# Moving weight forms, conversions, chunk-end sums, evacuations and seeds in a Fourier-mixing and gated-FFN kernel

## Chip, cores and metric

The kernel runs on one core of one Trainium2 chip. The metric is the device time of one execution in microseconds; the median of three runs is given. The engines are called TensorE (PE in the profile; PEld is its weight load), VectorE (DVE), ScalarE (ACT), GpSimd (POOL) and SyncE (SP, which issues most DMAs).

## What is computed

The reference is a Fourier mixing of eight sequences of 3008 tokens with 256 features, followed by a gated feed-forward layer:

```python
X = np.fft.fft(x, axis=1)            # x: (8, 3008, 256)
X = np.fft.fft(X, axis=2)
y = X.real.astype(np.float32).reshape(8 * 3008, 256)
gate = 1.0 / (1.0 + np.exp(-(y @ w_gate)))     # w_gate, w_val: (256, 1536)
val = y @ w_val
out = (gate * val @ w_out).astype(np.float32)  # w_out: (1536, 256)
```

The weights arrive as 64-bit floats, so the kernel converts them to 32 bits itself; everything is computed in 32-bit floats.

## The kernel before

**The mixing.** The transform over the features is merged into the gate and value weights (`merge`, giving G1 and G2), so that the sequence transform alone is left per batch. It uses symmetry: x is folded (`fold_ops`), then multiplied by a table of cosines and sines (`seq_group`, `whole`), giving the parts pk and qk of a spectrum of 1505 positions. A position k and its mirror S-k have the same two products with opposite signs, so a gate or value at k is P + Q and at S-k it is P - Q.

**The main loop.** The 1505 positions are cut into six chunks of 252 (the last is 246), for each of eight batches. A chunk meets 12 tiles of 128 hidden units, so there are 48 chunks of 12 steps, 576 steps i in all. In step i the program emits, in this order:

- `front_a(i)`: two products with pk into a PSUM bank PF[i], two matmuls each. From step 12 on the bank was *seeded* before, by ScalarE (`seed`, L501), with the part of the outcome that is of rank one.
- `gate_a(i-1)`: ScalarE's sigmoid for position k (L534, into h) and VectorE's z for position S-k (L536 or L539).
- `part(i)`: the copy ae of PF[i], by ScalarE (L515) from step 12 on and by VectorE (L518) before. `front_b(i)` adds to the same bank, so it waits for ae.
- `gate_b(i-1)`: gate times value at k on VectorE (L551), the S-k sigmoid on ScalarE (L552), their product on VectorE (L553), and, after the second and third tile of a group of three, seven and six *h sums* on GpSimd (L558).
- the uses of weights due in this step (`use`): merges of gate and value weights on TensorE, evacuated to G2 and G1 by ScalarE; for output weights that complete a group, `forms(g)`.
- `back`: five of the fifteen products of an earlier group with the output weight forms, into the PSUM banks po0 to po4.
- `front_b(i)`: two products with qk.
- then the ScalarE half of a weight conversion (`weight_parts`, L260 and L261), the seed of step i+2, up to three items of the list `later`, and last the side work: VectorE's and GpSimd's half of a conversion (`weight_join`, L270 to L273, L275), weight loads, folds of the next batch's x on GpSimd, sequence groups.

A group of three hidden tiles is one level of a bilinear scheme: 15 products in place of 18, paid for by the h sums, by sums of the output weights (`W_SUMS`, eleven, and four copies per group, made once), and by 20 sums of the outcome at the end of each chunk (`C_SUMS`, L604). `back` works on group p five to seven steps after its first tile.

**At the end of a chunk** the banks po0 to po4 are copied to the tile c as they complete (L582), then `finish` puts 20 sums, four transposes (L612) and the stores into `later`, from where three go out per step. The first three go out in step 4 of the next chunk (counted from 0), the last in step 11. After the last chunk all of this is emitted at once, from a list of its own (`C_LAST`) whose entries also name the engine.

**What sets the order.** The program order above is each engine's order; nothing is rescheduled. Each engine works through its own list and waits where an operand, or a buffer to be written, isn't ready. PF has three banks, h three buffers, z, ae and sf two, c one. The weight jobs j run from 0 to 17 (gate, value and output weights by pairs of hidden tiles): job j >= 9 is converted in step j-9; gate and value pairs are merged two or three steps after that, and the output weights of groups 0 to 3 are formed in steps 3, 5, 9 and 11.

Of the kernel before, what the change touches and what calls it, by code (L numbers as in the profile page):

```python
# [11 lines left out]
ALU = mybir.AluOpType  # L12
# [49 lines left out]
PRODUCTS = ((0, 12), (1, 11), (4, 9), (6, 4), (2, 13), (5, 5), (13, 0), (8, 6), (11, 2), (12, 8), (9, 3),  # L62
            (10, 10), (14, 1), (15, 7), (16, 14))
PLACE = (0, 1, 2, 5, 3, 4, 6, 7, 8, 9, 10, 11, 14, 13, 12)
C_SUMS = (((8, 1, 8, 0), (1, 1, 0, 0), (3, 3, 1, 0), (0, 0, 10, 1), (4, 4, 0, 1), (1, 6, 2, 0),
           (4, 4, 1, 0), (10, 14, 8, 1), (7, 7, 10, 0), (11, 0, 11, 0), (11, 11, 5, 0), (5, 5, 7, 1)),
          ((9, 9, 8, 0), (9, 13, 9, 1), (9, 9, 2, 0), (12, 9, 12, 0), (12, 11, 12, 1), (14, 9, 14, 0),
           (6, 11, 6, 0), (13, 13, 6, 1)))
OUT = (3, 12)

C_LAST = (((8, 1, 8, 0), 0), ((1, 1, 0, 0), 0), ((3, 3, 1, 0), 0), ((1, 6, 2, 0), 1), ((0, 0, 10, 1), 0),
          ((11, 0, 11, 0), 1), ((4, 4, 0, 1), 0), ((4, 4, 1, 0), 0), ((11, 11, 5, 0), 1),
          ((9, 9, 8, 0), 1), ((10, 14, 8, 1), 0), ((7, 7, 10, 0), 0), ((6, 11, 6, 0), 1),
          ((5, 5, 7, 1), 0), ((9, 13, 9, 1), 0), ((9, 9, 2, 0), 0), ((14, 9, 14, 0), 0),
          ((13, 13, 6, 1), 0), ((12, 9, 12, 0), 0), ((12, 11, 12, 1), 0))
HUGE = float((2 ** 24 - 1 - 2 ** 20) * 2.0 ** -7)


@with_exitstack
def kernel(  # L80
# [174 lines left out]
    def weight_parts(j):  # L255

        if j in RAW:
            raw, ws = RAW[j], WS[j]
            lo, hi = raw[:, :, :, 0], raw[:, :, :, 1]
            nc.scalar.activation(ws, hi.bitcast(F32), AF.Abs)  # L260
            nc.scalar.activation(lo, lo.bitcast(U32), AF.Copy, scale=2.0 ** -29)  # L261

    def weight_join(j):
        if j not in RAW:
            return
        raw, ws = RAW.pop(j), WS[j]
        lo, hi = raw[:, :, :, 0], raw[:, :, :, 1]
        wi = ws.bitcast(I32)
        ts = nc.vector.tensor_scalar
        ts(out=ws, in0=ws, scalar1=2.0 ** -15, scalar2=HUGE, op0=ALU.max, op1=ALU.min)  # L270
        ts(out=wi, in0=wi, scalar1=3, scalar2=0x3FFFFFF8, op0=ALU.logical_shift_left,
           op1=ALU.bitwise_and)
        nc.vector.scalar_tensor_tensor(out=wi, in0=hi, scalar=-(2 ** 30), in1=wi,  # L273
                                       op0=ALU.bitwise_and, op1=ALU.bitwise_or)
        nc.gpsimd.tensor_tensor(wi, wi, lo, op=ALU.add)  # L275

    WO = {}

    def weight_use(j, other=None):
        w, c = jobs[j]  # L280
        if w == 2:
            WO[c] = WS.pop(j)
            for g in range(NG):
                if (3 * g + 2) // 2 == c:
                    forms(g)
        else:
            merge(WS.pop(j), w, c, other)

# [13 lines left out]
    def forms(g):  # L302

        w = [WO[f // 2].rearrange("p f (a h j) -> p f h a j", h=2, j=TB)[:, f % 2]
             for f in range(3 * g, 3 * g + 3)]
        f = wf[:, g].rearrange("p m (a j) -> p m a j", j=TB)

        def block(i):
            return w[i // 2][:, i % 2] if i < 6 else f[:, i - 6]
        for i, (a, b, op) in enumerate(W_SUMS):  # L310
            nc.gpsimd.tensor_tensor(f[:, i], block(a), block(b), op=(ALU.subtract, ALU.add)[op])  # L311
        for i, (a, sign) in enumerate(W_COPIES):
            nc.scalar.mul(f[:, len(W_SUMS) + i], block(a), float(sign))


    W = {}
# [224 lines left out]
    def block(p, i):  # L541

        R = 2 * chunks[groups[p][1]][1] // 3
        return H[p][:, i % 3, i // 3 * R : (i // 3 + 1) * R] if i < 9 else SF[p][:, i - 9, 0:R]
# [20 lines left out]
    def back(p, part):  # L565

        b, c, g = groups[p]
        n = chunks[c][1]
        R = 2 * n // 3
        last = p == len(groups) - 1  # L570
        if part == 0 and g == 0:
            PO[:] = [pso.tile([P, 2 * WC], F32, name=f"po{t}", tag=f"po{t}") for t in range(NB)]
        for at_, (hb, wb) in list(enumerate(PRODUCTS))[part * 5 : part * 5 + 5]:
            t, j = divmod(PLACE[at_], 3)
            mm(PO[t][:, j * R : (j + 1) * R], wf[:, g, wb], block(p, hb), g == 0 and at_ % 3 == 0,
               g == NG - 1)
            if g == NG - 1 and at_ % 3 == 2:
                if t == 0:
                    C[0] = cp.tile([P, 10 * WC], F32, name="c", tag="c")
                    nc.gpsimd.memset(C[0][:, 15 * R : 15 * R + 40], 0.0)  # L580
                if not (last and t == NB - 1):
                    nc.scalar.copy(C[0][:, 3 * t * R : 3 * (t + 1) * R], PO[t][:, 0 : 3 * R])  # L582
        if part == 2:
            del H[p], SF[p]
            if g == NG - 1:
                finish(b, c, last)

    def finish(b, c, last):
        k0, n = chunks[c]
        R = 2 * n // 3  # L590
        more = k0 + n > NK
        nb = -(-n // TB)
        t = C.pop(0)
        queues = (nc.sync, nc.scalar) if last else (nc.sync,)
        os_ = []

        new = set()

        def sum_(dst, a, b, op, engine=nc.vector):

            there = lambda i: last and i >= 3 * (NB - 1) and i not in new
            v = [PO[NB - 1][:, (i - 3 * NB + 3) * R : (i - 3 * NB + 4) * R] if there(i) else
                 t[:, i * R : (i + 1) * R] for i in (a, b)]
            engine.tensor_tensor(t[:, dst * R : (dst + 1) * R], *v, op=(ALU.subtract, ALU.add)[op])  # L604
            new.add(dst)

        def flip(s, h):
            if not os_:
                os_.append(op.tile([P, NK + 1], F32, name="os", tag="os")[:, 0 : 4 * WC].rearrange(
                    "p (s b h j) -> p s b h j", s=2, h=2, j=TB))  # L610
            c0 = OUT[h] * R + (n + more if s else 0)
            nc.vector.transpose(os_[0][:, s, 0:nb, h, :], t[:, c0 : c0 + nb * TB])  # L612

        def store(s):
            m, r0 = (min(n, M - k0), b * S + k0) if s == 0 else (
                n - (k0 == 0) - more, b * S + S - k0 - n + 1 + more)
            full = m // TB
            for a in range(4):
                ps = slice(a * TB, (a + 1) * TB)
                cs = slice(a * 2 * TB, (a + 1) * 2 * TB)  # L620
                queues[a % len(queues)].dma_start(
                    out=out[r0 : r0 + full * TB, cs].rearrange("(b t) d -> t b d", t=TB),
                    in_=os_[0][ps, s, 0:full].rearrange("p b h j -> p b (h j)"))
                if m > full * TB:
                    queues[a % len(queues)].dma_start(out=out[r0 + full * TB : r0 + m, cs],
                                      in_=os_[0][a * TB : a * TB + m - full * TB, s, full].rearrange(
                                          "p h j -> p (h j)"))

        if last:
            for x, e in C_LAST:  # L630
                sum_(*x, engine=(nc.vector, nc.gpsimd)[e])
                if x[0] == 5:
                    flip(0, 0)
                    flip(1, 0)
            for half in range(2):
                flip(half, 1)
                store(half)
            return
        for h in range(2):
            later.extend([lambda x=x: sum_(*x) for x in C_SUMS[h]])  # L640
            later.append(lambda h=h: flip(0, h))
            later.append(lambda h=h: (flip(1, h), h and (store(0), store(1))))

# [49 lines left out]
    def at(i, *fs):  # L695
        side.setdefault(i, []).extend(fs)
# [2 lines left out]

    pre, use = {}, {}  # L700
    for j in range(9, len(jobs)):
        pre.setdefault(j - 9, []).append(lambda j=j: weight_parts(j))
        at(j - 9, lambda j=j: weight_join(j))
        if KEEP <= j < len(jobs) - 3:
            at(j - 9, lambda j=j: weight_load(j + 3))
    for j in range(3, len(jobs)):
# [40 lines left out]
    for i in range(count):  # L747
        front_a(i)
        if i:
            gate_a(i - 1)  # L750
        part(i)
        if i:
            gate_b(i - 1)
        for f in use.pop(i, []):
            f()
        if i >= 5:
            back((i - 5) // 3, (i - 5) % 3)
        front_b(i)
        for f in pre.pop(i, []):
            f()  # L760
        for j in range(max(i0, i + 1), min(count, i + 3)):
            if j not in PF:
                seed(j)
        for f in later[0:3]:
            f()
        del later[0:3]
        for f in side.pop(i, []):
            f()
# [55 lines left out]
```

## Time and profile before

| | |
|---|---|
| median of 3 runs (lowest to highest) | 1994.02 us (1992.43 to 1995.59) |
| span of the profiled run, mean granted clock of TensorE | 1993.0 us, 0.993 |
| chain of work that ended last: PE, DVE, ACT, POOL | 79%, 12%, 5%, 2% |
| its largest lines | PE pf 40%, PE po 33%, DVE c L604 6% |
| VectorE's chunk-end sums (L604) | 950, 0.564 us each |
| GpSimd's h sums (L558) | 2496 |
| ScalarE's chunk-end evacuations (L582) | 239, 0.574 us each |
| ScalarE's seeds (L501) | 1128, 0.475 us each |

"Busy" is the time in which an engine had an instruction in work. In an instruction group `out<-in` gives the tiles by their names in the program; "idle before" is the time that the engine stood still just before, and the arrow names the instruction that ended it. All products go through one helper, so TensorE's rows have its line, L131, and are told apart by tiles: pf<-pk is front_a, pf<-qk front_b, po is back, ps a merge, ev and od the sequence transform.

### The profile page before, as it was taken

How to read it: one execution, taken by the hardware profiler on the slowest of the kernel's cores; microseconds unless marked ns; L12 is line 12 of the kernel's file. 1: busy time of each engine (PE TensorE's matmuls, PEld its weight loads, DVE VectorE, ACT ScalarE, POOL GpSimd, SP SyncE). 2: the span in 40 equal slices, each digit the busy share in tenths (PEclk: the TensorE clock that was granted, in tenths of full speed). 3: DMA queues.
4: the chain of work that ended last, by engine and by line, in shares of the span. 5: the costliest groups of instructions: out<-in, count | busy, mean ns of one | idle time of the engine just before them, and what ended most of it. 6: DMA issues, size and time to landing. Idle time of an engine off the chain costs nothing.

```text
span 1993.0 us, 34353 instructions
## 1 busy us (share of the span) xinstructions
PE 1945.6 (98%) x11232; PEld 1793.0 (90%) x11232; DVE 1538.4 (77%) x3061; ACT 1395.6 (70%) x3198; POOL 1627.1 (82%) x2878
## 2 busy tenths in 40 slices
PE   6799999999999999999999999999999999999997
PEld 4689889998999899998999989999899999999997
DVE  7668778886788778787878877788678876877776
ACT  3467767776777667776777767777677776777775
POOL 3788988897888878897889878888788886777776
PEclk8999999999999999999999999999999999999999
DMA  7253413112012020211112021111210110011011
GB/s 266 86 132 90 139 29 109 45 25 80 14 46 56 16 77 14 60 44 49 43 25 79 15 77 24 45 49 20 79 19 14 20 21 14 14 23 18 14 21 24
DMA packets 171414, 101.40 MB, mean 51 GB/s; under 512 B 133860, under 2 KB 163172, under 8 KB 168556
## 3 DMA queue, kind: packets, MB, share of 16 engines
q1 hardware_dynamic: 169294, 98.64, 19.7%
q8 instruction: 88, 1.44, 0.3%
q10 hardware_dynamic: 1940, 0.56, 0.1%
q14 instruction: 92, 0.75, 0.1%
HBM read 74.39 MB, written 50.18 MB: 63 GB/s over the span
## 4 chain that ended last, share of the span: by engine, by line
PE 79%; DVE 12%; ACT 5%; POOL 2%; issue 1%; DMA 1%; SPq 0%; POOLq 0%; DVEq 0%; ACTq 0%
PE pf L131 40%; PE po L131 33%; DVE c L604 6%; PE ev L131 4%; DVE z L539 3%; DVE h L553 2%; ACT z L552 2%; ACT pf L501 1%; PE od L131 1%; ACT ae L515 1%; DMA x<-in_xf_dram 1%; POOL wf L311 1%; ACT c L582 1%; POOL sf L558 1%; PE ps L131 1%
## 5 line engine op out<-in xcount | busy, mean ns | idle before, releaser
L558 POOL TENSOR_TENSOR sf<-h 128x168 f32<-128x168 f32 (+1 forms) x960 | 540.4, 581 | 239.3 <-DVE h L553 239.3
L558 POOL TENSOR_TENSOR sf<-h,sf 128x168 f32<-128x168 f32 (+1 forms) x1152 | 644.9, 579 | 56.1 <-DVE h L553 56.1
L131 PE MATMUL pf<-qk,G 128*128 128x252 f32 (+1 forms) x2304 | 587.8, 378 | 7.7 <-DVE ae L518 4.3
L131 PE MATMUL pf<-pk,G 128*128 128x252 f32 (+1 forms) x2304 | 582.7, 376 | 0.0
L501 ACT ACTIVATE pf<-ek,ge 128x252 f32<-128x252 f32 (+1 forms) x1128 | 535.8, 475 | 18.4
L539 DVE TENSOR_TENSOR z<-ae,pf 128x504 f32<-128x504 f32 (+1 forms) x564 | 376.5, 668 | 221.2 <-ACT h L534 220.5
L604 DVE TENSOR_TENSOR c<-c 128x168 f32<-128x168 f32 (+1 forms) x950 | 520.9, 564 | 16.9 <-ACT c L582 3.6
L131 PE MATMUL po<-sf,wf 128*128 128x168 f32 (+1 forms) x3072 | 530.9, 306 | 0.0
L131 PEld LDWEIGHTS pf<-pk,G 128*128 128x128 f32 x2304 | 437.1, 190 | 51.8 <-issue 2.3
L131 PE MATMUL po<-h,wf 128*128 128x168 f32 (+1 forms) x2688 | 477.2, 306 | 6.2 <-POOL wf L311 4.6
L131 PEld LDWEIGHTS po<-sf,wf 128*128 128x128 f32 x3072 | 473.9, 190 | 8.4
L131 PEld LDWEIGHTS po<-h,wf 128*128 128x128 f32 x2688 | 428.2, 190 | 23.6 <-POOL wf L311 5.1
L131 PEld LDWEIGHTS pf<-qk,G 128*128 128x128 f32 x2304 | 408.3, 190 | 44.8 <-ACT ae L515 12.5
L515 ACT ACTIVATE ae<-pf 128x504 f32<-128x504 f32 (+1 forms) x564 | 331.0, 587 | 147.6 <-PE pf L131 142.1
L553 DVE TENSOR_TENSOR h<-z 128x252 f32<-128x252 f32 (+1 forms) x576 | 335.7, 583 | 115.7 <-ACT z L552 114.5
L552 ACT ACTIVATE z<-z 128x252 f32<-128x252 f32 (+1 forms) x576 | 236.2, 410 | 217.8 <-DVE z L539 194.0
L534 ACT ACTIVATE h<-pf 128x252 f32<-128x252 f32 (+1 forms) x576 | 213.2, 370 | 81.7 <-PE pf L131 68.7
L551 DVE TENSOR_TENSOR h<-h,pf 128x252 f32<-128x252 f32 (+1 forms) x576 | 233.1, 405 | 0.0
L582 ACT COPY c<-po 128x504 f32<-128x504 f32 (+1 forms) x239 | 127.5, 574 | 2.9 <-PE po L131 2.9
L558 POOL TENSOR_TENSOR sf<-sf 128x168 f32<-128x168 f32 (+1 forms) x192 | 109.7, 571 | 15.0
L558 POOL TENSOR_TENSOR sf<-sf,h 128x168 f32<-128x168 f32 (+1 forms) x192 | 112.8, 588 | 0.0
L131 PE MATMUL ev<-st,x 63*128 63x376 f32 (+4 forms) x372 | 98.1, 416 | 7.6 <-DVE x L335 7.6
(103 smaller groups left out, 793.6 us busy)
## 6 DMA issues: line engine op xcount, KB each, us to landing
x<-xr SPq DMA_DIRECT2D x14, 1536.0 KB
out_dram<-os SPq DMA_DIRECT2D x380, 56.0 KB
xr<-in_xf_dram SPq DMA_DIRECT2D x14, 768.0 KB
xr<-in_xf_dram SPq DMA_DIRECT2D x35, 256.0 KB
ek<-ed SPq DMA_DIRECT2D x39, 126.0 KB
out_dram<-os SPq DMA_DIRECT2D x288, 7.0 KB
x<-in_xf_dram SPq DMA_DIRECT2D x2, 1512.0 KB
tr<-in_stab_dram SPq DMA_DIRECT2D x2, 1129.5 KB
```

The lines of the kernel that those rows point to most:

```text
L131: nc.tensor.matmul(o, l, r, start=start, stop=stop, skip_group_check=True)
L311: nc.gpsimd.tensor_tensor(f[:, i], block(a), block(b), op=(ALU.subtract, ALU.add)[op])
L501: nc.scalar.activation(PF[i][:, g], EK[i // NFT], AF.Copy, scale=ge[:, g, f : f + 1])
L515: nc.scalar.activation(AP[i], PF[i], AF.Copy, scale=2.0)
L534: nc.scalar.activation(H[p][:, fh, 0:n], PF[i][:, 0], AF.Sigmoid)
L539: nc.vector.tensor_tensor(z[:, :, ::-1], AP.pop(i), PF[i], op=ALU.subtract)
L551: nc.vector.tensor_tensor(h[:, fh, 0:n], h[:, fh, 0:n], PF.pop(i)[:, 1], op=ALU.mult)
L552: nc.scalar.activation(z[:, 0], z[:, 0], AF.Sigmoid)
L553: nc.vector.tensor_tensor(h[:, fh, n:], z[:, 0], z[:, 1], op=ALU.mult)
L558: nc.gpsimd.tensor_tensor(block(p, dst), block(p, a), block(p, b), op=(ALU.subtract, ALU.add)[op])
L582: nc.scalar.copy(C[0][:, 3 * t * R : 3 * (t + 1) * R], PO[t][:, 0 : 3 * R])
L604: engine.tensor_tensor(t[:, dst * R : (dst + 1) * R], *v, op=(ALU.subtract, ALU.add)[op])
```

## The change

Five things are moved; the arithmetic stays as it was.

1. **Output weight forms in halves.** `forms(g)` gives back two pieces of work, of six sums (and the four copies) and of five. They wait in the list `parts_`, from which one goes out per step. Groups 0 and 1 stay on GpSimd, groups 2 and 3 go to VectorE, so that VectorE makes half of them.
2. **Conversions mid-step.** Both halves of a conversion are emitted together, between `gate_b(i-1)` and `back`: ahead of the step's merges and of newly completed forms, but behind a piece of forms that was left over from the step before.
3. **Some chunk-end sums on GpSimd.** The order and the engines of `C_LAST` now serve every chunk: five of the 20 sums are GpSimd's. The first transposes come after the fourteenth sum, the others and the stores at the end.
4. **Some evacuations on VectorE.** po1 and po3 are copied to c by VectorE, po0, po2 and po4 by ScalarE.
5. **Seeds ahead of the S-k sigmoid.** In step i the bank of step i+1 is seeded, between `part(i)` and `gate_b(i-1)`; before, that of step i+2 at the end of the step.

Items 1 and 2 are for the first 16 steps, where GpSimd's list mixes h sums, forms and conversions. Items 3 and 4 spread the chunk end over three engines, and item 5 lets ScalarE do the seeds while it would wait for VectorE's z.

```diff
-C_SUMS = (((8, 1, 8, 0), (1, 1, 0, 0), ...
-C_LAST = (((8, 1, 8, 0), 0), ((1, 1, 0, 0), 0), ((3, 3, 1, 0), 0), ((1, 6, 2, 0), 1), ((0, 0, 10, 1), 0),
+C_SUMS = (((8, 1, 8, 0), 0), ((1, 1, 0, 0), 0), ((3, 3, 1, 0), 0), ((1, 6, 2, 0), 1), ((0, 0, 10, 1), 0),
           ((11, 0, 11, 0), 1), ((4, 4, 0, 1), 0), ((4, 4, 1, 0), 0), ((11, 11, 5, 0), 1),
           ((9, 9, 8, 0), 1), ((10, 14, 8, 1), 0), ((7, 7, 10, 0), 0), ((6, 11, 6, 0), 1),
           ((5, 5, 7, 1), 0), ((9, 13, 9, 1), 0), ((9, 9, 2, 0), 0), ((14, 9, 14, 0), 0),
           ((13, 13, 6, 1), 0), ((12, 9, 12, 0), 0), ((12, 11, 12, 1), 0))
...
-                    forms(g)
+                    parts_.extend(forms(g))
...
+        engine = nc.gpsimd if g < 2 else nc.vector
...
-        for i, (a, b, op) in enumerate(W_SUMS):
-            nc.gpsimd.tensor_tensor(f[:, i], block(a), block(b), op=(ALU.subtract, ALU.add)[op])
-        for i, (a, sign) in enumerate(W_COPIES):
-            nc.scalar.mul(f[:, len(W_SUMS) + i], block(a), float(sign))
+        def some(lo, hi):
+            for i, (a, sign) in enumerate(W_COPIES if lo == 0 else ()):
+                nc.scalar.mul(f[:, len(W_SUMS) + i], block(a), float(sign))
+            for i, (a, b, op) in list(enumerate(W_SUMS))[lo:hi]:
+                engine.tensor_tensor(f[:, i], block(a), block(b), op=(ALU.subtract, ALU.add)[op])
+        return [lambda lo=lo: some(lo, lo + 6) for lo in range(0, len(W_SUMS), 6)]
...
-                    nc.scalar.copy(C[0][:, 3 * t * R : 3 * (t + 1) * R], PO[t][:, 0 : 3 * R])
+                    (nc.vector.tensor_copy if t % 2 else nc.scalar.copy)(
+                        C[0][:, 3 * t * R : 3 * (t + 1) * R], PO[t][:, 0 : 3 * R])
...
-        for h in range(2):
-            later.extend([lambda x=x: sum_(*x) for x in C_SUMS[h]])
-            later.append(lambda h=h: flip(0, h))
-            later.append(lambda h=h: (flip(1, h), h and (store(0), store(1))))
+        for x, e in C_SUMS:
+            add(lambda x=x, e=e: sum_(*x, engine=(nc.vector, nc.gpsimd)[e]))
+            if x[0] == 5:
+                add(lambda: flip(0, 0))
+                add(lambda: flip(1, 0))
+        for half in range(2):
+            add(lambda half=half: (flip(half, 1), store(half)))
...
-        pre.setdefault(j - 9, []).append(lambda j=j: weight_parts(j))
-        at(j - 9, lambda j=j: weight_join(j))
+        pre.setdefault(j - 9, []).append(lambda j=j: weight_round(j))
...
         part(i)
+        if i0 <= i + 1 < count:
+            seed(i + 1)
         if i:
             gate_b(i - 1)
-        for f in use.pop(i, []):
+        todo = pre.pop(i, []) + use.pop(i, [])
+        for f in [parts_.pop(0)] + todo if parts_ else todo + [lambda: parts_ and parts_.pop(0)()]:
             f()
         if i >= 5:
             back((i - 5) // 3, (i - 5) % 3)
         front_b(i)
-        for f in pre.pop(i, []):
-            f()
-        for j in range(max(i0, i + 1), min(count, i + 3)):
-            if j not in PF:
-                seed(j)
         for f in later[0:3]:
             f()
```

Here an entry (dst, a, b, op) of `C_SUMS` makes part dst from parts a and b of c, by a difference (0) or a sum (1), and the number after it is the engine: 0 VectorE, 1 GpSimd.

## The prediction

> **What bounds the kernel now.** First the page's busy list, then the stretches, then who TensorE waited for. The first line says that TensorE has 2% to give.
>
> ```profile
> PE 1945.6 (98%) x11232; PEld 1793.0 (90%) x11232; DVE 1538.4 (77%) x3061; ACT 1395.6 (70%) x3198; POOL 1627.1 (82%) x2878
> ```
>
> The stretches (us, then busy time of PE, PEld, DVE, ACT, POOL, then the granted clock) show where. From 60 to 120 us, steps 2 to 13 with the weight conversions, PE lacks 13.6 us and POOL is busy for 54.6 of 60; from 160 to 1960 PE lacks only 5 of 1800.
>
> ```profile
> 60.00:120.00 60.00, 46.39 (x217) 40.46 (x217) 37.64 (x73) 26.26 (x72) 54.59 (x95) 0.91 0.30 92
> 160.00:1960.00 1800.00, 1795.05 (x10514) 1665.22 (x10513) 1402.51 (x2800) 1305.36 (x2988) 1498.24 (x2665) 1.00 0.17 42
> ```
>
> PE's own waits name GpSimd twice in that early stretch: an integer add that ends a weight conversion (L275), and the output weight forms (L311).
>
> ```profile
> PE ps L131 <- POOL wx L275: 5.5, 1, 5.5
> PE po L131 <- POOL wf L311: 4.6, 2, 2.9
> ```
>
> In the timeline (start, length, engine, line) the eleven form sums run in one piece, and the add that TensorE needs stands behind them; the eight merge matmuls after the wait then take 3.78 us instead of 1.89 (at 97.58).
>
> ```profile
> 87.21 0.63 POOL L311 TENSOR_TENSOR wf<-wx 128x128 f32<-128x128 f32 x1
> ...
> 88.63 1.27 POOL L275 TENSOR_TENSOR wx<-wx 128x512 int32<-128x512 int32 x1
> ...
> 89.95 3.78 PE L131 MATMUL ps<-wx,dt 128*128 128x256 f32 x8 [5.51 <-POOL wx L275]
> ...
> 97.58 1.89 PE L131 MATMUL ps<-wx,dt 128*128 128x256 f32 x8
> ```
>
> Later a quiet step takes 3.12 us from one front_a to the next (119.32 to 122.45). Where VectorE has three chunk-end sums in a step it needs more than that:
>
> ```profile
> 343.31 0.67 DVE L539 TENSOR_TENSOR z<-ae,pf 128x504 f32<-128x504 f32 x1
> 343.90 0.40 DVE L551 TENSOR_TENSOR h<-h,pf 128x252 f32<-128x252 f32 x1
> 344.46 0.61 DVE L553 TENSOR_TENSOR h<-z 128x252 f32<-128x252 f32 x1 [0.15 <-ACT z L552]
> 344.99 1.84 DVE L604 TENSOR_TENSOR c<-c 128x164 f32<-128x164 f32 x3
> 346.75 0.67 DVE L539 TENSOR_TENSOR z<-ae,pf 128x504 f32<-128x504 f32 x1
> ```
>
> That is 3.44 us from z to z, and front_a follows suit: 343.67, 347.17, 350.61. The PE wait is hidden in the modelled ends, so I took the spacing of front_a over all steps: outside the sequence groups and the one step with e_sums, 12.9 us lie above 3.12, all in steps 7 to 12 of chunks whose GpSimd also folds x. That is the second thing to win.
>
> **What the Trainium skill says.** "SBUF — State Buffer", Who interferes with whom: VectorE and GpSimd share a pair of SBUF ports under an exclusive lock. The trace agrees: a c sum takes 0.33 us at 1973.64 with GpSimd idle, 0.564 in the mean. "GPSIMD Engine Reference", Engine selection: a two-input operation is about twice as slow there as on VectorE; here 0.58 against 0.33 at the end, near equal under contention. "TensorE: Matmul & The Clock Gate", What's actually happening: after an idle window of some 3.4 us the clock falls to half. Here 5.51 us did that, 2.89 slowed the next matmuls too (six po in 2.04 us, 1.12 after the 1.69 us wait).
>
> **The change, part by part.** T is step time; "lag" is how late VectorE's z is behind the sigmoid that feeds it.
>
> *Conversions mid-step.* ScalarE's two conversion passes (0.68 + 0.67) go ahead of the G copies that wait for the merge. In step 0 VectorE's L270 waited until 53.30; now it can start when ae ends, 51.2. Following VectorE (z 0.67, ae 0.86, h 0.41 + 0.6, conversion 2.0) from there, z of steps 1 to 3 comes 1.4 to 1.9 us earlier, and so does the h that starts GpSimd's second set of sums (66.44, I take 64.5).
>
> *Forms six a step, half on VectorE.* GpSimd's order from 66.44 was: 6 h sums, 11 forms, two adds, 7 h sums, 11 forms, add 14, 6 h sums, add 15 (ends 94.23). The new order on GpSimd holds the same operations, add 12 ahead of the first forms, add 14 ahead of the second forms, add 15 behind all. So add 14, waited for at 89.95, ends at about 64.5 + 3.9 + 1.3 + 5.7 + 1.3 + 4.3 + 1.3 = 82.3, before TensorE asks (82.9): that wait goes. But GpSimd has no idle time to drop: add 15 ends at 94.2 - 1.9 = 92.3, and TensorE, without the first wait, asks for it at 88.0 in step 8. **The wait moves on one step**, 4.3 us long, with the same slow clock behind it: 5.9 us from merge to front_b as at 89.95 to 95.88. front_b of step 8 then starts at 98.3 instead of 100.74. Also the first forms end no sooner (1.9 gained, add 12 put ahead, 1.3): step 5 still waits for them, which the later wait swallows.
> Forms 2 and 3 on VectorE: 22 sums. No row shows them; 0.29 us is the bound below (0.33 scaled from 168 to 128 columns) and 0.45 above (GpSimd's own 0.44 to 0.45). I take 0.40. Six are 2.4 us in step 9, five 2.0 in step 10; behind them in VectorE's queue stand z and ae, and front_b waits for ae: about 1.7 + 1.2 us lost. In exchange the 2.89 us wait for L311 at 112.97, its slow clock (0.9 + 0.55), and 0.4 before front_b at 104.42 go. From front_b 8 to front_a 12 took 15.5 us (100.74 to 116.20); I get 13.1. Steps 11 and 12 are past the ae on VectorE and hide the rest. Start: 2.4 + 2.4, **4.7 us won** after rounding down.
>
> *Seeds ahead of the S-k sigmoid.* Between z and the next ae ScalarE now has 0.41 + 0.36 + 0.58 us, no longer two seeds of 0.48 as well. At 343.98 z ended, ae at 346.16, and front_b (due 345.94) started 0.27 late: z could be 1.62 us late at no cost. It can now be about 2.5 late. The seed comes a step later but still over 2 us ahead of its front_a: nothing.
>
> *Sums and evacuations.* Five of 20 sums a chunk go to GpSimd (+2.85 us at 0.57), two evacuations to VectorE (0.6 each: the 504 column copy takes ScalarE 0.574, the 504 column z takes VectorE 0.67). VectorE: -2.8 + 1.2 a chunk; ScalarE -1.15, hidden. The evacuations are needed two steps later: nothing. Steps with three sums become steps with one or two, so the 3.44 us steps go (up to 12.9 us). But now **VectorE waits for GpSimd**: the second (4,4) sum reads what GpSimd makes of 1; (5,5) overwrites what GpSimd's (11,11) reads; and the second transpose reads four columns into part 6, which GpSimd's (6,11) writes. These stand behind GpSimd's h sums. Behind the waiting sum or transpose on VectorE stands the next z; ScalarE's sigmoid of it waits for that, behind it the next h sigmoid and ae, and TensorE's front_b for ae. For each chunk I took the end of the h sums ahead of each from the trace, added 0.57 for each new sum and took off idle time in between. z after the transpose comes 1.4 to 2.0 us late in most chunks (below 2.5 even with 0.4 more from the next three sums), but folds make GpSimd late: at 433.76 it still ran the h sums of a step begun at 428.8. With 0.5 us off for less contention, chunks of batch 0 lose 2.5, 3.7, 1.9, 0.8 and 0.8, and five later chunks 0.9 each: 14.2 us against the 12.9 there are. **1.3 us lost.**
>
> *The end.* VectorE's copy of bank 3 (PE ends it at about 1980.3) now stands ahead of its first three sums, which began at 1980.18: 0.8 us lost.
>
> Sum: 1994.0 - 4.7 + 1.3 + 0.8 = **1991.4**.
>
> **Rivals.** *The late sums fit (faster).* If GpSimd speeds up more once VectorE runs fewer sums (h sums took 0.60 in 410 to 440, 0.52 at best: eighteen of them would save 1.4 us, not 0.5) only some 5 of the 12.9 us remain: 1994.0 - 4.7 - 7.9 + 0.8 = 1982.2. For it: VectorE is the slower one in those steps. Against: GpSimd is busy 38 of 40 us at 400 to 440 and gets work.
> *VectorE behind GpSimd (slower).* No relief at all: every late chunk loses 0.5 more, five more begin to lose (21.2 us against 12.9), and forms on VectorE at 0.45 or more with slow clocks leave 2 of the 4.7: 1994.0 - 2 + 8.3 + 0.8 = 2001.1. A z that may be only 1.6 late would be worse still.
>
> **How the numbers follow.** Forecast 0.46, the faster rival 0.33, the slower 0.21. The range takes in nearly all of the first two and half of the third: 1981 to 2001. Faster by over 0.2% (below 1990.0): the rival and a third of the forecast's spread of 3 us, 0.49. Slower (above 1998.0): most of the third, 0.20. Same: 0.31.
>
> **What would show it.** Right: no wait for the conversion near 85 to 90 us but one of about 4 us one step on; no PE wait for forms near 113; c sums on POOL; VectorE idle ahead of L604 or the transposes with POOL as the releaser, longest near 270 and 434 us; front_a spacing of 3.12 in most steps. Wrong: no wait for add 15 (start worth 8 us or more), no VectorE wait for POOL, or PE spacings over 3.12 in chunks without folds.

## The result, and the profile after

The changed kernel takes **2021.75 us** (median of 4 runs, 2019.79 to 2026.29); the kernel before took 1994.8 beside it (4 runs, 1992.43 to 1995.91). The ratio is 1.014, with a 95% interval of 1.012 to 1.016: slower. The prediction said 1991.4, in a range up to 2001.0.

Line numbers shift with the change: the helper of all products is now L127, the chunk-end sums are L605, the transposes L613, the forms L312, the conversions L266 to L271. First the page of the changed kernel, its busy line and the chain that ended last (shares of the span by engine):

```profile
PE 1954.1 (97%) x11232; PEld 1788.8 (89%) x11232; DVE 1487.4 (74%) x2944; ACT 1320.3 (65%) x3102; POOL 1737.5 (86%) x3091
...
PE 61%; POOL 25%; DVE 7%; ACT 2%; DMA 2%; issue 2%; POOLq 0%; SPq 0%; ACTq 0%; DVEq 0%
```

VectorE and ScalarE have been relieved, as intended. But POOL, 2% of the chain before, is now 25% of it. The two stretches of the prediction, in the same columns:

```profile
60.00:120.00 60.00, 50.02 (x244) 43.96 (x243) 50.59 (x99) 28.03 (x77) 52.03 (x82) 0.94 0.32 93
160.00:1960.00 1800.00, 1777.43 (x10357) 1636.24 (x10356) 1323.95 (x2626) 1212.10 (x2849) 1591.39 (x2853) 1.00 0.17 42
```

In the early stretch PE gained 3.6 us of work (50.02 for 46.39). In the long one it lost 17.6 of 1800 (1777.43 for 1795.05), where before it had lacked only 5 in all. What VectorE waited for (total us, times, longest):

```profile
DVE h L553 <- ACT z L552: 311.4, 561, 1.3
DVE c L605 <- POOL c L605: 49.7, 31, 3.9
DVE os L613 <- POOL c L605: 47.7, 46, 1.4
```

The second and third line are new: 97.4 us in which VectorE stands in front of a sum or a transpose because GpSimd's sum isn't done. TensorE's own waits, also in us, times and longest:

```profile
PE pf L127 <- ACT ae L515: 19.9, 35, 3.1
...
PE po L127 <- POOL wf L312: 3.3, 1, 3.3
PE ps L127 <- ACT G L293: 2.9, 1, 2.9
```

The early waits of before (5.5 us for a conversion, 1.7 and 2.9 for forms) have become one of 3.3 us for the first forms and one of 2.9 in step 8. But front_b waits for ScalarE's ae 35 times, up to 3.1 us; before, it did so twice, up to 0.9 us. The longest of these waits stands just ahead of 433.1, and for the 3.4 us behind it the granted clock was 0.50:

```profile
433.10:436.50 3.40, 3.40 (x8) 2.82 (x9) 3.21 (x7) 1.56 (x4) 3.32 (x7) 0.50 0.00 0
```

There is one more such stretch between 120 and 1960 us, from 211.2 to 214.6; the kernel before has none. How much of the loss they make wasn't measured by itself.

**Where the time went.** I took the time of each front_a in both traces. The profiled span grew by 25.0 us. Of that, 2.5 is a later first front_a (a table load; in the profiled runs of the experiments this point came 0.4 to 3.9 us later than before whatever was changed, so it is scatter). From front_a(0) to front_a(12) the change won 6.1. From front_a(12) to the last it lost **27.3**, and 1.4 behind it. Of the 27.3, 10.6 are in chunks 1 to 9 and 16.7 in the five batches from chunk 10 to chunk 39, all in chunks whose GpSimd also folds x. From chunk 40 on, without folds, nothing is lost.

**One such chunk.** VectorE in chunk 14 of the changed kernel; at the end of a line in brackets the idle time just before it and what ended it:

```profile
670.16 0.66 DVE L605 TENSOR_TENSOR c<-c 128x168 f32<-128x168 f32 x1
672.26 0.65 DVE L605 TENSOR_TENSOR c<-c 128x168 f32<-128x168 f32 x1 [1.44 <-POOL c L605]
672.84 0.67 DVE L539 TENSOR_TENSOR z<-ae,pf 128x504 f32<-128x504 f32 x1
...
679.47 0.78 DVE L553 TENSOR_TENSOR h<-z 128x252 f32<-128x252 f32 x1 [0.15 <-ACT z L552]
681.68 0.45 DVE L613 STREAM_TRANSPOSE os<-c 128x256 f32<-128x256 f32 x1 [1.43 <-POOL c L605]
682.05 0.88 DVE L605 TENSOR_TENSOR c<-c 128x168 f32<-128x168 f32 x2
682.86 0.67 DVE L539 TENSOR_TENSOR z<-ae,pf 128x504 f32<-128x504 f32 x1
```

A sum is named by its entry (dst, a, b), so (4,4,1) is the second (4,4) sum. At 672.26 it has waited for GpSimd's (1,6,2), at 681.68 the second transpose for GpSimd's (6,11,6). Both times z stands behind. GpSimd in the same chunk:

```profile
671.68 1.04 POOL L605 TENSOR_TENSOR c<-c 128x168 f32<-128x168 f32 x2
...
677.16 2.32 POOL L558 TENSOR_TENSOR sf<-h 128x168 f32<-128x168 f32 x4
679.44 1.22 POOL L558 TENSOR_TENSOR sf<-h,sf 128x168 f32<-128x168 f32 x2
680.61 0.54 POOL L558 TENSOR_TENSOR sf<-h 128x168 f32<-128x168 f32 x1
681.11 0.54 POOL L605 TENSOR_TENSOR c<-c 128x168 f32<-128x168 f32 x1
...
687.96 1.06 POOL L558 TENSOR_TENSOR sf<-h 128x168 f32<-128x168 f32 x2 [1.76 <-DVE h L553]
```

(6,11,6) at 681.11 stands behind seven h sums, 4 us of work. From 652.5 to 686.2 GpSimd stands still for no more than 0.1 us at a time; then it has caught up and waits 1.76 us for the next h, as it did at the same place in the kernel before (1.76 us, at 676.67). On VectorE the late z goes on to ScalarE's S-k sigmoid:

```profile
683.55 0.41 ACT L552 ACTIVATE z<-z 128x252 f32<-128x252 f32 x1 [2.19 <-DVE z L539]
```

and by the next h sigmoid and ae to TensorE's front_b:

```profile
684.77 1.12 PE L127 MATMUL pf<-qk,G 128*128 128x252 f32 x4 [0.36 <-ACT ae L515]
```

front_a follows in steps of 3.75 and 3.45 us instead of 3.12. TensorE's modelled ends show only 0.36 of that as a wait, which is why the spacing was used. The first wait costs nothing in this chunk: front_a keeps to 3.12 until the second. In chunk 13, where z comes 3.8 us late behind (4,4,1), that step takes 4.19 us.

### The profile page after: what moved, and what is told of

Same layout as the page of the kernel before. It is cut to its first block, busy times and chain, and to the rows that moved or that the text cites. A ratio compares the mean times of both kernels' runs of the same rounds, so it can differ in the third digit from the quotient of the medians.

```text
span 2018.0 us, 34483 instructions
## 1 busy us (share of the span) xinstructions
PE 1954.1 (97%) x11232; PEld 1788.8 (89%) x11232; DVE 1487.4 (74%) x2944; ACT 1320.3 (65%) x3102; POOL 1737.5 (86%) x3091
## 4 chain that ended last, share of the span: by engine, by line
PE 61%; POOL 25%; DVE 7%; ACT 2%; DMA 2%; issue 2%; POOLq 0%; SPq 0%; ACTq 0%; DVEq 0%
PE pf L127 31%; PE po L127 25%; POOL sf L558 17%; PE ev L127 4%; POOL c L605 3%; DVE c L605 3%; POOL x L338 2%; DVE z L539 2%; DVE h L553 1%; POOL x L354 1%; ACT z L552 1%; DMA st<-in_stab_dram 1%; DVE os L613 1%; POOL x L325 1%; DMA ge<-G 1%
## 5 line engine op out<-in xcount | busy, mean ns | idle before, releaser
L127 PE MATMUL pf<-qk,G 128*128 128x252 f32 (+1 forms) x2304 | 590.8, 379 | 24.3 <-ACT ae L515 19.9
L553 DVE TENSOR_TENSOR h<-z 128x252 f32<-128x252 f32 (+1 forms) x576 | 356.2, 618 | 312.0 <-ACT z L552 311.4
L127 PE MATMUL pf<-pk,G 128*128 128x252 f32 (+1 forms) x2304 | 584.8, 377 | 0.0
L127 PE MATMUL po<-sf,wf 128*128 128x168 f32 (+1 forms) x3072 | 530.6, 306 | 0.0
L127 PEld LDWEIGHTS pf<-pk,G 128*128 128x128 f32 x2304 | 432.5, 190 | 59.0 <-ACT pf L501 3.9
L127 PE MATMUL po<-h,wf 128*128 128x168 f32 (+1 forms) x2688 | 477.5, 306 | 5.3 <-POOL wf L312 3.3
L127 PEld LDWEIGHTS po<-sf,wf 128*128 128x128 f32 x3072 | 472.9, 190 | 8.9 <-POOL sf L558 0.6
L127 PEld LDWEIGHTS pf<-qk,G 128*128 128x128 f32 x2304 | 409.5, 191 | 66.2 <-ACT ae L515 35.7
L127 PEld LDWEIGHTS po<-h,wf 128*128 128x128 f32 x2688 | 429.0, 191 | 22.7 <-POOL wf L312 3.6
L605 DVE TENSOR_TENSOR c<-c 128x168 f32<-128x168 f32 (+1 forms) x715 | 390.4, 556 | 58.2 <-POOL c L605 49.7
L534 ACT ACTIVATE h<-pf 128x252 f32<-128x252 f32 (+1 forms) x576 | 215.1, 373 | 106.5 <-PE pf L127 92.4
L605 POOL TENSOR_TENSOR c<-c 128x168 f32<-128x168 f32 (+1 forms) x240 | 133.1, 571 | 1.3 <-DVE c L605 1.2
L613 DVE STREAM_TRANSPOSE os<-c 128x256 f32<-128x256 f32 x192 | 79.1, 431 | 49.3 <-POOL c L605 47.7
```

The lines of the kernel that those rows point to most:

```text
L127: nc.tensor.matmul(o, l, r, start=start, stop=stop, skip_group_check=True)
L534: nc.scalar.activation(H[p][:, fh, 0:n], PF[i][:, 0], AF.Sigmoid)
L553: nc.vector.tensor_tensor(h[:, fh, n:], z[:, 0], z[:, 1], op=ALU.mult)
```

## The experiments

The theories: **A**, GpSimd's five sums (its load, or VectorE's waiting for them); **B**, the seeds, which delay L553; **C**, the evacuations, which fill VectorE. The times of runs that were made together share a kernel before at 1995 to 1996 us; ratios to it have their 95% interval in brackets. "Steady" is what was won or lost from front_a(12) to the last front_a in the profiled run, against before. The expectations of some runs speak of seven GpSimd sums a chunk; that was a slip of mine, there are five.

**The parts one by one.** Seeds put back:

```diff
-        if i0 <= i + 1 < count:
-            seed(i + 1)
...
+        for j in range(max(i0, i + 1), min(count, i + 3)):
+            if j not in PF:
+                seed(j)
```

> The changed kernel with item 5 undone: seeds again of step i+2 at the end of the step. Its trace has the product h of S-k (L553) end 2.9 us after the h sigmoid starts in quiet steps, 2.0 before the change, so GpSimd's h sums start 0.9 us later. Theory A (GpSimd is loaded to the brim by the chunk-end sums and VectorE waits for it; the seeds matter little): 2015 to 2022 us. Theory B (the seeds, by delaying L553 and with it GpSimd, turned a harmless wait into a loss): most of the 27 us comes back, 1993 to 2003. I lean to a mixture, about 2010.

Measured: 2021.92 us, 1.0138 [1.0105, 1.017]. B falls: with the seeds put back the loss is the same.

The chunk-end sums back on VectorE, the last chunk left alone:

```diff
-            add(lambda x=x, e=e: sum_(*x, engine=(nc.vector, nc.gpsimd)[e]))
+            add(lambda x=x, e=e: sum_(*x, engine=(nc.vector, nc.gpsimd)[e and last]))
```

> The changed kernel with all chunk-end sums of the first 47 chunks on VectorE, in the new order; the last chunk as it was. Theory A: VectorE no longer waits for GpSimd, the loss goes, 1990 to 1997 us. Theory B (seeds): GpSimd's h sums stay 0.9 us later, most of the loss stays, 2010 or more. Theory C (the evacuations overload VectorE at the chunk's end): VectorE now has 20 sums and two copies, the loss grows, above 2022.

Measured: 1999.4 us, 1.0018 [1.001, 1.0026]. Some 22 us come back; steady loss 6.3 instead of 27.3. The cause lies in the five sums, with a smaller rest elsewhere.

The kernel before with items 1 and 2 alone, and with item 5 alone (the diffs are those parts of the change):

> The kernel before with items 1 and 2 alone: forms in halves, half on VectorE, conversions mid-step. The changed kernel's front_a of step 12 comes 6.1 us earlier after its step 0 than before. If that belongs to these two items, 1994.8 minus 4 to 6: 1989 to 1991. If part of it came from elsewhere, less than 3 us.

> The kernel before with item 5 alone: seeds ahead of the S-k sigmoid. Prediction's step: z may be 2.5 us late instead of 1.6, so part of the 12.9 us of VectorE-bound steps goes: 1985 to 1994. Theory B: L553 comes 0.9 us later, GpSimd falls behind in chunks with folds: over 2000.

Measured: 1990.36 us, 0.9968 [0.9956, 0.998], with 6.1 us won up to step 12 and nothing later; and 1991.77 us, 0.9973 [0.9959, 0.9987], steady gain 2.8. Both parts help by themselves.

On top of the sums on VectorE, the evacuations back on ScalarE (e5); and these alone put back in the changed kernel (e6):

```diff
-                    (nc.vector.tensor_copy if t % 2 else nc.scalar.copy)(
+                    (nc.scalar.copy)(
```

> The changed kernel with all sums of the first 47 chunks on VectorE and all evacuations on ScalarE again: of items 3 and 4 only the new order of the sums (and both transposes of a half behind each other) is left, beside the start and the seeds. Theory A (what is lost is GpSimd's load and VectorE's waits for its sums): the start's and the seeds' gains stand alone, some 4.5 and 3.5 us, so about 1987 to 1989 us where before is at 1995. Theory C (the evacuations on VectorE also cost): this is clearly below the kernel with the sums alone moved back (1999.4), by 8 us or more; if that kernel's remaining loss was the new order of the sums, this one stays at 1996 to 2000.

> The changed kernel with the evacuations of the chunk ends on ScalarE again, GpSimd's seven sums kept. Theory A (GpSimd is late under the folds, VectorE waits at (4,4), (5,5) and the second transpose): the lateness of GpSimd stays, so most of the loss does: 2012 to 2020 us. Theory C (VectorE is overloaded by the evacuations, which make the sums late): 1995 to 2003 us.

Measured: e5 1988.98 us, 0.9962 [0.9951, 0.9974]; e6 2019.48 us, 1.0114 [1.0074, 1.0154]. The evacuations cost 10 us where VectorE has all the sums (1999.4 against 1989.0). In the changed kernel the difference is 2.3 us, which the intervals don't tell from nothing. The start and the seeds without any other item, in the old order of the sums:

> The kernel before with items 1, 2 and 5 alone (forms and conversions at the start, seeds ahead of the sigmoid of S - k; old order of the sums). The gains of the two single runs added, 6.4 and 5.4 us by their ratios, would give 1983 to 1985 us; the kernel that has the new order beside these gave 1989.0, so if the order is neutral, 1987 to 1990 us, and if it costs, 1983 to 1986 us.

Measured: 1988.87 us, 0.9962 [0.9947, 0.9976]. As e5: the new order by itself costs nothing, and the gains of the parts add up only in part.

**Does it need the folds?** They were left out of both kernels (`for i, f in enumerate(ops[:0])`).

> The changed kernel with the folds of G of batches 1 to 7 left out (that part of the computation is missing: each later batch uses what lies in the buffers). It takes from GpSimd and VectorE the work that fills them in batches 0 to 6 and leaves the rest. Theory A says the loss needs the folds beside GpSimd's sums: this kernel then takes the time of the kernel before without folds, or up to 8 us less. A rival, that GpSimd's sums cost by the wait of VectorE alone whatever else GpSimd has to do: still some 20 us above it.

> The kernel before with the same folds left out (that part of the computation is missing). It is the yardstick for the run ahead of it. Chunks with folds cost the kernel before some 13 us of spacing above 3.12 us a step, by its trace; without them I expect 1980 to 1986 us.

Measured: 1978.75 us, 0.9912 [0.9885, 0.994], and 1981.11 us, 0.9924 [0.9898, 0.9949]. The loss is gone: outside the same few long steps that both have (those around e_sums, and the start of a batch), every step from the second chunk on takes 3.12 us or a little less. (All these folds are GpSimd's; VectorE has none of them.) From front_a(12) to the last, the folds cost the kernel before 13.1 us and the changed kernel 40.3. VectorE still waits at the transposes without folds, for less long, and it costs nothing:

```profile
DVE os L613 <- POOL c L605: 23.7, 47, 0.9
```

**Load or wait?** Was GpSimd simply full? In e9 VectorE has its sums, and GpSimd runs one on a spare tile for each of the five. In e10 GpSimd does 8 of the 168 columns of its sums and VectorE the other 160.

```diff
+        def spare():
+            nc.gpsimd.tensor_tensor(idle[:, 0:R], idle[:, 2 * WC // 3 : 2 * WC // 3 + R],
+                                    idle[:, 2 * WC // 3 : 2 * WC // 3 + R], op=ALU.add)
...
-            add(lambda x=x, e=e: sum_(*x, engine=(nc.vector, nc.gpsimd)[e]))
+            add(lambda x=x, e=e: (sum_(*x, engine=(nc.vector, nc.gpsimd)[e and last]),
+                                   e and not last and spare()))
...
```

```diff
+            if engine is nc.gpsimd and not last:
+                nc.vector.tensor_tensor(o[:, 8:], v[0][:, 8:], v[1][:, 8:], op=op)
+                o, v = o[:, :8], [x[:, :8] for x in v]
+            engine.tensor_tensor(o, *v, op=op)
...
```

> The changed kernel with all chunk-end sums of the first 47 chunks on VectorE (as in the run that gave 1999.4), while GpSimd runs a sum of the same shape on a spare tile in each place where it had a real one: GpSimd's load without VectorE's waits. Theory A1 (GpSimd is full: 38.2 to 39.2 us of work in chunks 12 to 14 where twelve steps of 3.12 us have 37.4, so each such chunk stretches to GpSimd's own time): 2016 to 2024 us, as the changed kernel. Theory A2 (VectorE, waiting in order for a late sum, delays the product z behind it): 1998 to 2003 us.

> The changed kernel with GpSimd doing only 8 of the 168 columns of each of its seven sums of the first 47 chunks and VectorE the other 160: VectorE's waits for GpSimd stay at the same three places, GpSimd's load almost goes (an estimate of 0.1 us a sum against 0.4 to 0.57). Theory A1: 1999 to 2005 us, near the kernel with the sums on VectorE. Theory A2: 2015 to 2025 us.

Measured: 2003.76 us, 1.0039 [1.0025, 1.0052]; and 2005.7 us, 1.0055 [1.0038, 1.0072]. The load alone costs 4 us of the 22. e10 misses its aim twice: a sum of 8 columns still took GpSimd 0.30 us, so that half of the load stayed, and with less to do GpSimd was also less late, so that VectorE's waits, which I had meant to keep, were 15 us instead of 97.

```profile
DVE c L610 <- POOL c L610: 14.8, 8, 3.1
```

Two sums only, on the kernel of e5, with (6,11,6) moved behind the transposes:

```diff
+C_POOL = ((9, 9, 8, 0), (6, 11, 6, 0))
...
+            add(lambda x=x, e=e: sum_(*x, engine=(nc.vector, nc.gpsimd)[e and (last or x in C_POOL)]))
```

> The kernel of 1989.0 us (start, seeds and new order; sums on VectorE, evacuations on ScalarE) with two sums a chunk, (9,9,8) and (6,11,6), on GpSimd, the second moved behind the first two transposes. By theory A1 GpSimd has 36.5 us or less of work in a chunk without its sums, so two sums of some 0.4 us fit in 37.4: 1985 to 1989 us. If GpSimd has no room even for these, 1991 to 1996 us.

Measured: 1995.26 us, 0.9998 [0.999, 1.0007]: 6 us lost against e5 for two sums. VectorE waited once per chunk (47 times, 36.5 us): (13,13,6) stands one step behind (6,11,6). That pointed at the distance between a GpSimd sum and the VectorE instruction that needs it.

**Distance.** e13 moves one entry of the list; e14 is e13 with ScalarE's evacuations, e15 is e5 with the load of e9.

```diff
-           ((11, 0, 11, 0), 1), ((4, 4, 0, 1), 0), ((4, 4, 1, 0), 0), ((11, 11, 5, 0), 1),
-           ((9, 9, 8, 0), 1), ((10, 14, 8, 1), 0), ((7, 7, 10, 0), 0), ((6, 11, 6, 0), 1),
+           ((11, 0, 11, 0), 1), ((4, 4, 0, 1), 0), ((11, 11, 5, 0), 1), ((9, 9, 8, 0), 1),
+           ((10, 14, 8, 1), 0), ((7, 7, 10, 0), 0), ((6, 11, 6, 0), 1), ((4, 4, 1, 0), 0),
```

> The changed kernel with its five GpSimd sums a chunk kept, but placed so that what VectorE does with them comes two or three steps later in its queue: (4,4,1) moves from two places behind (1,6,2)'s step to step 8 of the chunk, and (11,11,5), (9,9,8), (6,11,6) go out up to one step sooner. GpSimd's load is the same, VectorE's waits are shortened. If the loss needs VectorE's wait (GpSimd alone carries a backlog on to the long step for G): most of it goes, 1998 to 2008 us. If GpSimd's load decides, or its lateness grows past two steps: 2014 to 2022 us.

> The same order with the evacuations on ScalarE again. If the wait decides: as the load alone on this base (the next run), some 1989 to 1998 us, since VectorE then has less to do than in any kernel so far. If load decides: 2010 to 2020 us.

> The kernel of 1989.0 us (start, seeds, new order, all sums on VectorE, evacuations on ScalarE) with GpSimd running five sums a chunk on a spare tile: its load alone, on a VectorE that has room. With the evacuations on VectorE the load alone cost 4 us; if that was the two engines taking turns on a full VectorE, it costs 0 to 3 here (1989 to 1992 us). If GpSimd's lateness with its h sums costs by itself: 1993 us or more.

Measured: e13 **1985.43 us**, 0.9952 [0.9936, 0.9969]; e14 1985.11 us, 0.9956 [0.9943, 0.9969]; e15 1992.68 us, 0.999 [0.9983, 0.9997]. e15 is 3.7 us above e5 (5.6 by the two ratios): the load alone costs some 4 us here too, more than expected. One entry is worth 36 us. (4,4,1) now goes out three steps behind (1,6,2), and (6,11,6) two steps ahead of the transpose, each one step in the changed kernel. (e13 changes both distances at once, and three of GpSimd's sums go out a step sooner with it.) VectorE's waits in e13:

```profile
DVE h L553 <- ACT z L552: 357.3, 560, 1.3
...
DVE c L605 <- POOL c L605: 13.3, 10, 3.6
```

The waits of the transposes and of (4,4,1) are gone. The ten that are left are all those of (5,5,7), which overwrites what GpSimd's (11,11,5) reads; these two stand two steps apart here as in the changed kernel. In e13's chunk 14 GpSimd does its last three sums of the chunk here:

```profile
661.92 1.90 POOL L605 TENSOR_TENSOR c<-c 128x168 f32<-128x168 f32 x3
```

and VectorE's second transpose comes without a wait, 1.7 us after they end:

```profile
665.52 0.43 DVE L613 STREAM_TRANSPOSE os<-c 128x256 f32<-128x256 f32 x1
665.88 0.89 DVE L605 TENSOR_TENSOR c<-c 128x168 f32<-128x168 f32 x2
666.70 0.67 DVE L539 TENSOR_TENSOR z<-ae,pf 128x504 f32<-128x504 f32 x1
```

That GpSimd was full is refuted as well. Chunk 14 as a stretch (columns as above, POOL the fifth busy time), first in the kernel before:

```profile
637.50:675.70 38.20, 38.09 (x217) 35.38 (x216) 31.21 (x61) 28.08 (x65) 33.45 (x59) 1.00 0.11 18
```

in the changed kernel:

```profile
647.20:685.70 38.50, 38.11 (x217) 35.13 (x217) 29.96 (x58) 26.54 (x63) 35.93 (x65) 1.00 0.11 18
```

and in e13:

```profile
633.80:671.30 37.50, 37.50 (x218) 35.34 (x217) 30.09 (x58) 27.38 (x64) 36.68 (x66) 1.00 0.12 19
```

POOL is busy for 35.93 of 38.50 us in the slow one and 36.68 of 37.50 in the fast one: there was room for the sums, and what the changed kernel loses comes of waiting.

Which of the two close pairs carries the loss? e16 parts the first one only, e17 frees the transpose only.

```diff
-           ((11, 0, 11, 0), 1), ((4, 4, 0, 1), 0), ((4, 4, 1, 0), 0), ((11, 11, 5, 0), 1),
-           ((9, 9, 8, 0), 1), ((10, 14, 8, 1), 0), ((7, 7, 10, 0), 0), ((6, 11, 6, 0), 1),
+           ((11, 0, 11, 0), 1), ((4, 4, 0, 1), 0), ((10, 14, 8, 1), 0), ((11, 11, 5, 0), 1),
+           ((9, 9, 8, 0), 1), ((4, 4, 1, 0), 0), ((7, 7, 10, 0), 0), ((6, 11, 6, 0), 1),
```

```diff
-           ((9, 9, 8, 0), 1), ((10, 14, 8, 1), 0), ((7, 7, 10, 0), 0), ((6, 11, 6, 0), 1),
-           ((5, 5, 7, 1), 0), ((9, 13, 9, 1), 0), ((9, 9, 2, 0), 0), ((14, 9, 14, 0), 0),
+           ((9, 9, 8, 0), 1), ((10, 14, 8, 1), 0), ((7, 7, 10, 0), 0),
+           ((5, 5, 7, 1), 0), ((6, 11, 6, 0), 1), ((9, 13, 9, 1), 0), ((9, 9, 2, 0), 0), ((14, 9, 14, 0), 0),
```

> The changed kernel with two of its chunk-end sums exchanged: (10,14,8) takes the place of (4,4,1), and (4,4,1), which waits for GpSimd's (1,6,2), stands a step later. GpSimd's sums stay where they were, and so does the wait of the second transpose for (6,11,6). In the changed kernel's trace the step with (4,4,1)'s wait and the one behind it are 13.7 us longer than before over the whole run, those of the transpose's wait 17.7 us. If each wait costs by itself, this saves 12 to 18 us: 2004 to 2010 us. If the waits feed each other (z late, h sums late, next wait longer), it saves more: below 2004. If it only moves the wait on to the transpose: 2016 to 2022 us.

> The changed kernel with (6,11,6) moved behind the first two transposes, so that the second transpose no longer waits for it; its own consumer (13,13,6) then comes a step behind it. The wait of (4,4,1) stays. If each wait costs by itself, this saves 14 to 20 us: 2002 to 2008 us. If the waits feed each other: below 2002. If (13,13,6) waits in its place: 2014 to 2022 us.

Measured: 2019.44 us, 1.0123 [1.0108, 1.0138]; and 2025.17 us, 1.015 [1.0133, 1.0167]. Neither alone helps; the loss moves to the next close pair. VectorE's waits in e16:

```profile
DVE os L613 <- POOL c L605: 61.5, 47, 1.9
DVE c L605 <- POOL c L605: 33.0, 28, 1.9
```

In e16 the steps that had been long through (4,4,1) are at 3.12 again (8 waits, 9.4 us in all, are left there; 20 waits, 23.5 us in all, are now at (5,5,7), and in chunks 4, 7 and 8 the steps behind them are some 4 us too long), and those behind the transpose have 26.5 us above it over the run, for 11.0 in the changed kernel. In e17 the transpose doesn't wait; (13,13,6), one step behind (6,11,6), does:

```profile
687.65 1.24 DVE L605 TENSOR_TENSOR c<-c 128x168 f32<-128x168 f32 x2 [1.56 <-POOL c L605]
```

and the first step of the next chunk has 20.5 us above 3.12 for 6.8 in the changed kernel. The kernels side by side ("apart": steps from (1,6,2) to (4,4,1) / from (6,11,6) to what first needs it):

| kernel | apart | VectorE's waits for POOL's sums, us | ratio to before |
|---|---|---|---|
| changed | 1 / 1 | 97.4 | 1.0140 |
| e16 | 2 / 1 | 94.5 | 1.0123 |
| e17 | 1 / 1 | 98.8 | 1.0150 |
| e13 | 3 / 2 | 13.3 | 0.9952 |
| e14, ScalarE evacuates | 3 / 2 | 14.7 | 0.9956 |
| e11, two sums only, ScalarE evacuates | - / 1 | 36.5 | 0.9998 |
| e2, no sums on GpSimd | none | 0 | 1.0018 |
| e9, the same with their load | none | 0 | 1.0039 |
| e5, no sums on GpSimd, ScalarE evacuates | none | 0 | 0.9962 |
| e15, the same with their load | none | 0 | 0.9990 |

The pair of (11,11,5) and (5,5,7) is two steps apart wherever GpSimd has five sums.

What stays open: whether a two-step distance at both close pairs would do as well as e13, and what would end the loss that e13 still has in one step each of chunks 4, 7 and 8, 4.4 us in all. There (5,5,7) waits 2.6 to 3.6 us for (11,11,5): where GpSimd folds most, two steps aren't always enough.

## Why the prediction was wrong

**The term that failed is "Sums and evacuations": 1.3 us lost as predicted, 27.3 measured. Within it, the step that failed is the time from which GpSimd's lateness was counted.** The mechanism was named: the same three instructions, the same seven h sums ahead, the same way by z, sigmoid and ae to front_b; the slower rival bore the name of what happened. The size was wrong by twenty times.

- *"It can now be about 2.5 late"* and *"I took the end of the h sums ahead of each from the trace"* don't go together. Item 5 lets z come some 0.9 us later, because the seeds are done ahead of the S-k sigmoid. For the same reason the product h of S-k (L553) comes later, and with it the h sums on GpSimd ahead of the five new sums. The gain was counted. The delay was not, because the h sums were taken from the trace of before, in which it isn't. The first L553 of chunk 14 in the kernel before, in e4 (item 5 alone) and in the changed kernel:

```profile
640.47 0.83 DVE L553 TENSOR_TENSOR h<-z 128x252 f32<-128x252 f32 x1 [0.15 <-ACT z L552]
642.29 0.82 DVE L553 TENSOR_TENSOR h<-z 128x252 f32<-128x252 f32 x1 [0.15 <-ACT z L552]
651.48 0.83 DVE L553 TENSOR_TENSOR h<-z 128x252 f32<-128x252 f32 x1 [0.15 <-ACT z L552]
```

They end 3.8, 4.7 and 5.1 us after the front_a of their step (at 637.51, 638.37 and 647.24). From chunk 40 on, where nothing is folded, it is 2.5, 3.5 and 3.6 us in the median.
- *"With 0.5 us off for less contention"*: not there. The Trainium skill ("SBUF — State Buffer", Who interferes with whom) has VectorE and GpSimd share a port pair under an exclusive lock, and I expected GpSimd to speed up as VectorE runs fewer sums. h sums take 0.578 us in the changed kernel and 0.581 before; VectorE's sums 0.556 and 0.564.
- What the two are worth can be estimated by doing the prediction's working again for all chunks, with the traces above. From the lines of chunk 14, z is taken to start 0.62 us after (1,6,2) ends and 1.21 after (6,11,6), and from quiet steps the sigmoid that feeds it to end 0.58 us after front_a. What z is late beyond the slack is lost, and a loss at the first wait shortens the second. These are estimates:

| GpSimd's h sums from the trace of | slack of z, us | off for less contention, us | lost in all chunks, us |
|---|---|---|---|
| before (the prediction's choice) | 2.5 | 0.5 | 13.4 (14.2 on record) |
| e4 | 2.5 | 0.5 | 26.2 |
| e4 | 2.5 | 0 | 35.4 |
| before | 1.6 | 0 | 36.1 |
| measured, with folds against without (e7) | | | 40.3 |

By these estimates the uncounted delay is worth some 13 us and the contention 9; the last 5 aren't traced to a cause (the working knows nothing of the slow clock near 433). The estimate of 36.1 leaves item 5 out altogether, its slack and its delay. That it comes to nearly the same fits e1, where undoing item 5 changed nothing: z behind the transpose is 2.2 us late there and may be 1.6.
- *"took off idle time in between"* held. In chunk 14 this working, on e4's h sums, has GpSimd end (6,11,6) 34.5 us after the chunk's first front_a; in the changed kernel it ended after 34.4. On the h sums of before it gives 33.5, and e1 has 33.5.
- *"z after the transpose comes 1.4 to 2.0 us late in most chunks"*: holds where nothing is folded. In the run without folds z starts 1.5 us after its h sigmoid ends in that step and 1.9 in the next, and it costs nothing. In most chunks with folds it is **3.1** behind the transpose in the changed kernel, and in the chunks that lose time there 2.9 to 6.0 behind (4,4,1)'s wait. The slack of 2.5 was right at the transpose: 3.15 - 2.5 gives 0.65, and the step was 0.62 us long too much.
- I weighed each wait by itself, chunk by chunk. But e16 and e17 show that GpSimd's lateness is paid at whichever close consumer comes next. *"five later chunks 0.9 each"* was 4.5 us; the five batches from chunk 10 lost 23.9 counted the same way (16.7 against the kernel before, which lost 7.2 there itself).
- *"The evacuations are needed two steps later: nothing"*: wrong on a VectorE with all its sums (10 us, e2 against e5), not to be told from nothing in the changed kernel (e6), and right in e13 against e14, where the sums have left VectorE. One copy took 0.67 us, not 0.6.
- *"so the 3.44 us steps go (up to 12.9 us)"* was a real gain: e13 has the sums on GpSimd, the evacuations on VectorE, and wins 5.2 us in its steady part where the changed kernel lost 27.3.

**The start was right, and a little small:** 4.7 us predicted, 6.1 measured up to step 12, 6.1 in e3 alone. The wait in step 8 came as forecast: the conversion's add ended at 94.87 (92.4 without the scatter ahead of it; predicted 92.3), and TensorE waited 2.9 us where 4.3 were forecast. That the add was named is in part luck. The profile puts the wait down to ScalarE's copy of G, which ended 0.12 us after the add and stood behind a conversion pass that had waited 5.1 us for GpSimd's forms; the prediction didn't see that path. Then front_b of step 8 started at 97.6 without the scatter (98.3 forecast), and no wait for forms is left near 113. A form sum on VectorE took 0.47 us in the mean, a little over the upper bound of 0.45, yet from that front_b to front_a(12) it was 12.5 us (13.1 forecast, 15.5 before).

**The end:** 0.8 predicted, 1.4 measured. **The seeds** were given nothing by themselves; on the kernel before they win 2.8 us from front_a(12) on (e4). In the changed kernel they win nothing (e1): the later L553 takes back what the slack gives.

In sum: 2.5 - 6.1 + 27.3 + 1.4 is the 25 us of the profiled spans. Of the prediction's error nearly all is one term.

## What to carry to other kernels

When work of one engine's in-order list is given to another engine whose list is nearly full, count the distance from producer to consumer in steps, not the free time on average: here one step apart cost 27 us, two to three steps won 5, with the same instructions. Work out the lateness in the stages where the receiving engine has most to do, and from a trace that already has the other changes in it: here one of them gave 0.9 us of slack and made the receiving engine 0.9 us later. A wait taken away at one place may be paid at the next, so look at all the consumers of the late engine together. Both rules come from this one kernel.

## What the runs showed of the hardware

GpSimd's sums of 128x168 took 0.571 us beside VectorE's 0.556, nearly the same price for both while both work; a sum of 128x8 still took GpSimd 0.296 us (e10). A copy of 504 columns out of a PSUM bank took VectorE 0.67 us and ScalarE 0.556, so the two copies that moved went to the dearer engine. A GpSimd busy for 36.68 of 37.50 us (e13) held TensorE up in no step of that chunk.
